# First dense layer of a two-layer transformer kernel: low weights of the last 64 features, two tiles in 64-row tiles of TensorE, and three PSUM banks dealt out by last use

## The chip, the cores and the metric

The kernel runs on one core of a Trainium2 chip. The metric is device time in microseconds (us), smaller is better. The kernel before takes 2498.18 us (median of three runs, 2494.75 to 2499.65). TensorE is PE in the profile, its weight loads are PEld, VectorE is DVE, ScalarE is ACT, GpSimd is POOL, and SP is the engine that issues most DMAs.

## The reference

Two transformer layers share one set of weights. Each is a linear attention with a learned softmax feature map, and a dense part with a squared ReLU:

```python
x = A_x                                                   # 1 x 2048 x 576
x = x + _A_ref(_layernorm(x, axis=-1), A_wqkv, A_w_phi, A_wo)
x = x + _B_ref(_layernorm(x, axis=-1), B_w1, B_b1, B_w2, B_b2)
x = x + _A_ref(_layernorm(x, axis=-1), A_wqkv, A_w_phi, A_wo)
x = x + _B_ref(_layernorm(x, axis=-1), B_w1, B_b1, B_w2, B_b2)

def _B_ref(x, w1, b1, w2, b2):                            # w1: 576 x 4608, w2: 4608 x 576
    h = jnp.einsum("bsd,df->bsf", x, w1) + b1
    r = jnp.where(h > 0, h, 0)
    h = r * r
    return jnp.einsum("bsf,fd->bsd", h, w2) + b2
```

The change touches only the first product of `_B_ref`, x @ w1.

## The kernel before

**Precision.** TensorE multiplies values of reduced precision (`float32r`) in one pass. Every factor is therefore split into a high and a low part, and a product is the sum of three: high by high, high by low, low by high.

**Blocks.** The 2048 rows are four blocks of 512 (`TB`). In the trace, `m_2ph` is the first product of block 2, both layers together. `g_mlp` is the dense part of one block and is called eight times: in layer 0 for the blocks 3, 2, 0, 1, in layer 1 for 1, 0, 3, 2. It is a generator, and `weave` runs one slot of other work (attention of the next block, norms, keys and values) after each of its `yield`s. The order on each engine is the order in which the program is written.

**Tiles of the dense part.** The 4608 hidden units are 36 tiles of 128 (`NF`). For a tile `f`, `hidden(f)` multiplies w1's columns by the transposed input and sums in a PSUM bank `ph`; `square(f)` applies ReLU and square on ACT (line 980 reads `ph`, line 981 squares in place in an SBUF tile `hr`) and splits the result on DVE into `hb` (lines 984 and 985); `second(f)` multiplies by w2 and sums in five banks `acc` that are held for the whole block (15 matmuls, lines 1000 and 992). On TensorE the order is hidden(f), second(f-1), hidden(f+1), second(f), and so on, with the slots of other work between them.

**The 576 features.** They are four chunks of 128 (`KC` = 4) and a rest of 64 (`DT`). `x["h"]` and `x["l"]` are the high and low input, features down the partitions. For the rest, `x["h"][:, KC]` holds the high part in one half of its 128 partitions and the low part in the other half. `load_twice` brings the 64 rows of w1 into both halves of the weight tile. So a matmul with the high weights `h1[:, KC]` gives high by high and high by low at once, and one with the low weights `l1[:, KC]` gives low by high, and low by low besides. A tile has 4 x 3 + 2 = 14 matmuls of 512 columns (line 975).

**Weights.** In the first block of layer 0 they are split on the chip and written to DRAM (`fresh`). In the seven others `first(f)` loads `h1` and `l1` of a tile in one DMA of 640 KB (line 938, on SP's queue), and `first2(f)` w2's (line 950, 576 KB). The tag `h1` has two buffers: the load for tile f+1 waits until hidden(f-1) has read its own.

**PSUM.** There are eight banks: five `acc`, one `h` for `ph` (except of f = 1), and a pool `ps_w` of two that `wtile` gives in turn to all other work.

Of the kernel before, what the change touches and what calls it, by code (L numbers as in the profile page):

```python
# [7 lines left out]
F32 = mybir.dt.float32  # L8
F32R = mybir.dt.float32r
AF = mybir.ActivationFunctionType  # L10
# [3 lines left out]
P = 128  # L14
TB = 512
# [6 lines left out]
def layers_kernel(  # L22
# [18 lines left out]
    nc = tc.nc  # L41
# [5 lines left out]
    NB = S // TB  # L47
    NF = F // P
    KC = D // P
    DT = D - KC * P  # L50
# [14 lines left out]
    ps_w = ctx.enter_context(tc.tile_pool(name="ps_w", bufs=2, space=bass.MemoryType.PSUM))  # L65
# [14 lines left out]


    spare = {"tags": [], "i": 0}

    def wtile(name):
        n = len(spare["tags"])
        spare["i"] += 1
        i = spare["i"] % (n + 2)
        if i < n:
            return ps_a.tile([P, TB], F32, tag=spare["tags"][i], name=name)
        return ps_w.tile([P, TB], F32, tag="w", name=name)  # L90

    def drain(gen):
        for _ in gen:
# [231 lines left out]
    class Norm:  # L325
# [62 lines left out]
        def rest(self, h):  # L388
            xh = self.dst["h"]
            rows = slice(h * TB // 2, (h + 1) * TB // 2)  # L390
            pt = wtile(f"{self.name}p{NT}{h}")
            for i in range(NT // 2):
                nc.tensor.transpose(pt[:DT, i * P : (i + 1) * P], self.xd[:, h * NT // 2 + i], ident)
            nc.scalar.activation(xh[:DT, KC, rows], pt[:DT, : TB // 2], AF.Copy)
            nc.vector.tensor_sub(xh[DT:, KC, rows], pt[:DT, : TB // 2], xh[:DT, KC, rows].bitcast(F32))

    class TripNorm(Norm):

# [55 lines left out]
        def rest(self, h):  # L454
            if not self.tails:
                return super().rest(h)
            xh = self.dst["h"]
            rows = slice(h * TB // 2, (h + 1) * TB // 2)
            own, far = (slice(i * DT, (i + 1) * DT) for i in (h, 1 - h))
            src = self.ends(h).rearrange("p (t g r) -> p t g r", t=2, g=KC)  # L460
            hi, lo = (xh[z, KC, rows].rearrange("p (t r g) -> p t g r", t=2, g=KC) for z in (own, far))
            nc.scalar.activation(hi, src, AF.Copy)
            nc.vector.tensor_sub(lo, src, hi.bitcast(F32))

    XT = (("h", xth, 0, KC // 2), ("l", xtl, 0, KC // 2), ("h", xth, KC // 2, NC), ("l", xtl, KC // 2, KC))

# [153 lines left out]
    def key_blocks(layer):  # L620
        kv = sums[layer]["kv"]
        last, w = NG - 1, gw[-1]
        kbh = cst.tile([GW, 2, D], F32R, name=f"kbh{layer}", tag="kbh")
        kbl = cst.tile([GW, 2, D], F32R, name=f"kbl{layer}", tag="kbl")
        sums[layer]["kb"] = kbh, kbl
        own = sb.tile([P, KC * P], F32, tag="xn", name=f"kq{layer}")
        own = own[:, : 2 * w].rearrange("p (s q f) -> p s q f", s=2, q=NQ)
        nc.vector.tensor_mul(own, kv[:, :, HG].unsqueeze(2).to_broadcast([P, 2, NQ, DH]),
                             quarter.unsqueeze(1).unsqueeze(3).to_broadcast([P, 2, NQ, DH]))
        blocks, todo = own, []  # L630

        def own_blocks():
            pt = wtile(f"kt{layer}2")
            p3 = pt[:w, : 2 * w].rearrange("p (s n) -> p s n", s=2)
            for s in range(2):
                nc.tensor.matmul(p3[:, s], blocks[:, s].rearrange("p q f -> p (q f)"),
                                 place.rearrange("p q d -> p (q d)"), start=True, stop=True)
            todo.append((p3, [k[:w, :, last * GW :] for k in (kbh, kbl)]))
            return todo

        for s in range(2):
            pt = wtile(f"kt{layer}{s}")
            nc.tensor.transpose(pt[:GW, :P], kv[:, s, :HG].rearrange("p j f -> p (j f)"), ident)
            own = sb.tile([P, TB], F32, tag="hr", name=f"ko{layer}{s}", bufs=2)
# [265 lines left out]
    def g_mlp(layer, b, x, after, name, fresh, apart, final):  # L910

        acc, parts, raw2 = [], {}, {}
        R = D - P
# [38 lines left out]

        every = slice(0, TB)

        def bank(f):
            parts[f] += (ps_w.tile([P, TB], F32, tag="w", name=f"{name}ph{f}") if f == 1 else
                         ps_a.tile([P, TB], F32, tag="h", name=f"{name}ph{f}"),)

        def hidden(f, cols):
            if len(parts[f]) == 3:  # L960
                bank(f)
            h1, l1, s2, ph = parts[f]
            xh, xl = x["h"], x["l"]
            todo = []
            for c in range(NC):
                ops = [(0, h1[:, c], xh[:, c, cols]), (1, l1[:, c], xh[:, c, cols])]
                if c < KC:
                    ops.insert(1, (0 if cols == every else 2, h1[:, c], xl[:, c, cols]))
                if c == KC and cols != every:
                    ops = [(3, *op[1:]) for op in ops]  # L970
                todo += ops
            if fresh or cols != every:
                todo.sort(key=lambda op: op[0])
            for k, (_, a, m) in enumerate(todo):
                nc.tensor.matmul(ph[:, cols], a, m, start=(k == 0), stop=(k == 3 * KC + 1))  # L975

        def square(f):
            s2, ph = parts[f][2:]
            hr = sb.tile([P, TB], F32, tag="hr", name=f"{name}hr{f}", bufs=2)
            nc.scalar.activation(hr, ph, AF.Relu, bias=b1t[:, f : f + 1])  # L980
# [28 lines left out]

        halves = (slice(0, TB // 2), slice(TB // 2, TB))  # L1010
        if apart:
            if fresh:
# [21 lines left out]
        second(0)  # L1034
        if fresh:
            load(3)
        first(2)
# [20 lines left out]
        yt = sb.tile([P, TB], F32, tag="hr", name=f"{name}yt", bufs=2)  # L1058
# [355 lines left out]
    def between(rows, held):  # L1414

        spare.update(tags=["h", "acc4", "acc1", "acc2", "acc3"], i=4)
        xprev, es, vpair, kpair = held["x"], held["es"], held["v"], held["k"]
        x = {}
        norm = Norm(x, "n1_last")
# [38 lines left out]
    def body():  # L1458
# [3 lines left out]
        for layer in range(2):  # L1462
            q1 = None
            ready, prev_rows, keep = {}, None, {}
            for i, b in enumerate(order):
                n = f"{layer}_{b}"
                nxt, rows = {}, []
                gen = g_mlp(layer, b, ready, rows, f"m{n}", layer == 0 and i == 0, i == 0, layer == 1 and i == NB - 1)
# [112 lines left out]
```

## Time and profile before

| | |
|---|---|
| median of 3 runs | 2498.18 us (2494.75 to 2499.65) |
| profiled execution | 2497.19 us, of which the span 2495.5 us |
| PE busy | 2478.5 us, 14968 matmuls |
| PEld busy | 2182.9 us |
| DVE, ACT, POOL busy | 1260.1, 788.1, 189.4 us |
| DMA | 545.07 MB, mean 218 GB/s |

The first number of a row of the timeline is the start in us from the start of the span, the second the length of the merged run, then engine, source line, operation, written tile <- read tiles, forms, and how many instructions were merged; in brackets stands the idle time of the engine just before it and what ended it. The time outside the span is 1.7 us.

### The profile page before, as it was taken

To read this page: it belongs to the slowest core of one execution; us is meant where nothing else is said; L and a number is where in the kernel's file an instruction comes from. 1 tells how busy PE (TensorE), PEld (TensorE's weight loads), DVE (VectorE), ACT (ScalarE), POOL (GpSimd) and SP (SyncE) were. 2 spreads that over 40 slices of the span, in tenths; PEclk is the share of its full clock that TensorE was granted. 3 is DMA by queue.
4 is the path that set the end of the run, shared out by engine and by line. 5 is a ranking of instruction groups with operands and counts; after the bars stand their busy time and mean duration, and the time that the engine had idled before them with its cause. 6 is when DMAs were issued, how large, how long until landed. Compare 5 with 4: busy or idle time off the path is not lost.

```text
span 2495.5 us, 37635 instructions
## 1 busy us (share of the span) xinstructions
PE 2478.5 (99%) x14968; PEld 2182.9 (87%) x14968; DVE 1260.1 (50%) x2214; ACT 788.1 (32%) x1439; POOL 189.4 (8%) x539
## 2 busy tenths in 40 slices
PE   9999999999999999999999999999999999999999
PEld 8999888888888888888888988888888888888887
DVE  6679885545744476455113776433453436442112
ACT  5444453422232223223213332413233222312212
POOL 4211100000200001000000011000110002000000
PEclk9999999999999999999999999999999999999999
DMA  9313698986767677684565248678576867676565
GB/s 321 98 54 92 243 315 266 310 315 205 259 229 271 217 206 273 216 298 146 195 199 182 92 141 263 209 217 291 186 257 204 261 219 246 217 230 230 194 199 171
DMA packets 214374, 545.07 MB, mean 218 GB/s; under 512 B 29006, under 2 KB 96814, under 8 KB 214198
## 3 DMA queue, kind: packets, MB, share of 16 engines
q1 hardware_dynamic: 163638, 500.44, 60.8%
q10 hardware_dynamic: 50560, 42.21, 5.3%
q8 instruction: 119, 1.95, 0.3%
q14 instruction: 57, 0.47, 0.1%
HBM read 439.20 MB, written 103.38 MB: 217 GB/s over the span
## 4 chain that ended last, share of the span: by engine, by line
PE 95%; DMA 2%; DVE 1%; ACT 1%; issue 1%; SPq 0%; ACTq 0%; DVEq 0%
PE m_1ph L975 9%; PE m_3ph L975 9%; PE m_0ph L975 9%; PE m_2ph L975 9%; PE m_1acc L1000 7%; PE m_3acc L1000 7%; PE m_2acc L1000 7%; PE m_0acc L1000 7%; PE m_1acc L992 2%; PE m_3acc L992 2%; PE m_2acc L992 2%; PE m_0acc L992 2%; PE a_0po L816 1%; PE a_2po L816 1%; PE kvp L593 1%; PE a_3po L816 1%
## 5 line engine op out<-in xcount | busy, mean ns | idle before, releaser
L975 PE MATMUL m_2ph<-a_2nh,m_2h 128*128 128x512 f32 x720 | 225.2, 394 | 1.2 <-ACT m_2hr L980 0.7
L975 PE MATMUL m_0ph<-a_0nh,m_0h 128*128 128x512 f32 x720 | 225.0, 394 | 1.3 <-ACT m_0hr L980 1.1
L1000 PE MATMUL m_3acc<-m_3s,m_3hb 128*128 128x448 f32 x864 | 189.3, 367 | 0.4 <-DVE m_3hb L984 0.4
L1000 PE MATMUL m_1acc<-m_1s,m_1hb 128*128 128x448 f32 x864 | 189.0, 367 | 0.3 <-PE m_1ph L975 0.3
L1000 PE MATMUL m_2acc<-m_2s,m_2hb 128*128 128x448 f32 x864 | 188.9, 367 | 0.0
L1000 PE MATMUL m_0acc<-m_0s,m_0hb 128*128 128x448 f32 x864 | 188.8, 367 | 0.0
L984 DVE CAST m_2hb<-m_2hr 128x512 fp32r<-128x512 f32 x72 | 31.2, 433 | 292.4 <-ACT m_2hr L981 292.3
L1000 PEld LDWEIGHTS m_1acc<-m_1s,m_1hb 128*128 128x128 f32 x864 | 161.9, 188 | 18.8 <-PE m_1ph L975 0.5
L1000 PEld LDWEIGHTS m_3acc<-m_3s,m_3hb 128*128 128x128 f32 x864 | 161.2, 188 | 17.8 <-PE m_3ph L975 0.6
L1000 PEld LDWEIGHTS m_2acc<-m_2s,m_2hb 128*128 128x128 f32 x864 | 161.6, 188 | 17.2
L1000 PEld LDWEIGHTS m_0acc<-m_0s,m_0hb 128*128 128x128 f32 x864 | 161.6, 188 | 17.2
L975 PEld LDWEIGHTS m_2ph<-a_2nh,m_2h 128*128 128x128 f32 x720 | 135.3, 188 | 32.7 <-ACT m_2hr L980 1.2
L975 PEld LDWEIGHTS m_0ph<-a_0nh,m_0h 128*128 128x128 f32 x720 | 135.2, 188 | 32.8 <-ACT m_0hr L980 1.5
L984 DVE CAST m_1hb<-m_1hr 128x512 fp32r<-128x512 f32 x72 | 30.7, 427 | 258.8 <-ACT m_1hr L981 258.8
L980 ACT ACTIVATE m_2hr<-m_2ph,b1t 128x512 f32<-128x512 f32 x72 | 49.6, 689 | 339.1 <-PE m_2ph L975 327.4
L980 ACT ACTIVATE m_1hr<-m_1ph,b1t 128x512 f32<-128x512 f32 x72 | 49.6, 689 | 319.1 <-PE m_1ph L975 309.1
L980 ACT ACTIVATE m_0hr<-m_0ph,b1t 128x512 f32<-128x512 f32 x72 | 49.6, 689 | 317.2 <-PE m_0ph L975 288.6
L984 DVE CAST m_0hb<-m_0hr 128x512 fp32r<-128x512 f32 x72 | 31.5, 438 | 229.0 <-ACT m_0hr L981 229.0
L984 DVE CAST m_3hb<-m_3hr 128x512 fp32r<-128x512 f32 x72 | 31.7, 440 | 173.6 <-ACT m_3hr L981 173.6
L980 ACT ACTIVATE m_3hr<-m_3ph,b1t 128x512 f32<-128x512 f32 x72 | 49.6, 689 | 219.3 <-PE m_3ph L975 209.2
L975 PE MATMUL m_3ph<-t0onh,m_3h 128*128 128x512 f32 (+1 forms) x380 | 112.9, 384 | 0.6 <-ACT t0onh L385 0.5
L975 PE MATMUL m_1ph<-t1onh,m_1h 128*128 128x512 f32 (+1 forms) x380 | 112.4, 382 | 0.8 <-ACT t1onh L385 0.5
(2050 smaller groups left out, 5734.9 us busy)
## 6 DMA issues: line engine op xcount, KB each, us to landing
m_2h<-dw SPq DMA_DIRECT2D x72, 640.0 KB
m_0h<-dw SPq DMA_DIRECT2D x72, 640.0 KB
m_1h<-dw SPq DMA_DIRECT2D x72, 640.0 KB
m_2s<-dw SPq DMA_DIRECT2D x72, 576.0 KB
m_0s<-dw SPq DMA_DIRECT2D x72, 576.0 KB
m_1s<-dw SPq DMA_DIRECT2D x72, 576.0 KB
dw<-m_3h SPq DMA_DIRECT2D x36, 640.0 KB
m_3h<-dw SPq DMA_DIRECT2D x36, 640.0 KB
```

The lines of the kernel that those rows point to most:

```text
L593: nc.tensor.matmul(po[32 * q : 32 * q + 32, :, j], vt[:, h * VW : h * VW + 32], e[:, :, h * DH : (h + 1) * DH], start=not stay, stop=True, ...
L816: nc.tensor.matmul(pt[:, :HP], a, m[:w, g], start=(g == 0 and k == 0), stop=(g == NG - 1 and k == 2))
L975: nc.tensor.matmul(ph[:, cols], a, m, start=(k == 0), stop=(k == 3 * KC + 1))
L980: nc.scalar.activation(hr, ph, AF.Relu, bias=b1t[:, f : f + 1])
L984: nc.vector.tensor_copy(hh, hr)
L992: nc.tensor.matmul(acc[KC], a, m, start=(f == 0 and k == 0), stop=(f == NF - 1 and k == 2))
L1000: nc.tensor.matmul(acc[t][:, :R], a[:, rows], m, start=(f == 0 and k == 0), stop=(f == NF - 1 and k == 2))
```

## The change

**Pairs.** For most even f from 2 on, `hidden(f)` leaves out the last matmul of its tile, the one with `l1[:, KC]`, and so does `hidden(f+1)`. In their place stand two matmuls at the end of hidden(f), one for each of the two tiles: 64 rows of weights each, the one for tile f in partitions 0 to 63, the one for f+1 in partitions 64 to 127. They write different banks. The low weights of both tiles multiply the high input alone; the product of low by low, which the matmul before gave besides, is left out in these tiles. Since the second of the two opens the sum of tile f+1, that tile's bank is taken, and its `l1` is read, at the end of hidden(f).

**The input of the pairs.** `twice` copies the high half of the last 64 features into both halves of a new tile `xt`, in four copies on POOL, once in a block, after second(0). `dst[h]` notes in which half the high part lies.

**Which tiles.** 17 pairs in each of the four blocks of layer 1, 16 (without f = 10) in the last three blocks of layer 0, none in its first: 116 pairs. 232 matmuls of 128 rows are replaced by 232 of 64.

**Banks and buffers.** `h` and the pool's two become three banks in a list; a taker gets the one whose last use was longest ago, `wtile` puts it back at once, `square` after its ReLU. `hr` has one buffer in place of two; `xt` has the room.

```diff
+    banks = ["w0", "w1"]
+
+    def take_bank(name):
+        tag = banks.pop(0)
+        return tag, ps_a.tile([P, TB], F32, tag=tag, name=name)
...
-        return ps_w.tile([P, TB], F32, tag="w", name=name)
+        tag, pt = take_bank(name)
+        banks.append(tag)
+        return pt
...
+        def twice():
+
+            xt = both["x"] = sb.tile([P, TB], F32R, tag="xt", name=f"{name}xt", bufs=1)
+            for h in range(2):
+                cols = slice(h * TB // 2, (h + 1) * TB // 2)
+                for i in range(2):
+                    nc.gpsimd.tensor_copy(xt[i * DT : (i + 1) * DT, cols], x["h"][x[h], KC, cols].bitcast(F32))
...
-        def hidden(f, cols):
-            if len(parts[f]) == 3:
+        def hidden(f, cols, pair=None):
+            if f not in ph:
                 bank(f)
...
+                elif pair is not None:
+                    ops.pop()
...
-                nc.tensor.matmul(ph[:, cols], a, m, start=(k == 0), stop=(k == 3 * KC + 1))
+                nc.tensor.matmul(ph[f][:, cols], a, m, start=(k == 0 and pair != 1), stop=(k == n and pair != 0))
+            if pair == 0:
+                bank(f + 1)
+                for i in range(2):
+                    rows = slice(i * DT, (i + 1) * DT)
+                    nc.tensor.matmul(ph[f + i], parts[f + i][1][rows, KC], both["x"][rows], start=(i == 1), stop=(i == 0))
...
-            hr = sb.tile([P, TB], F32, tag="hr", name=f"{name}hr{f}", bufs=2)
-            nc.scalar.activation(hr, ph, AF.Relu, bias=b1t[:, f : f + 1])
+            hr = sb.tile([P, TB], F32, tag="hr", name=f"{name}hr{f}", bufs=1)
+            nc.scalar.activation(hr, ph.pop(f), AF.Relu, bias=b1t[:, f : f + 1])
             nc.scalar.activation(hr, hr, AF.Square)
+            banks.append(held.pop(f))
...
-            hidden(f, every)
+            hidden(f, every, 0 if f in pairs else 1 if f - 1 in pairs else None)
...
+                pairs = [f for f in range(2, NF, 2) if layer or i and f != 10]
```

PE of block 2 in layer 0, from the last matmuls of hidden(2) to the first of hidden(3); `ph2` and `ph3` are the sums of these tiles, `h` and `l` behind `a0_2n` the high and low input, `h1_2` the weights of tile 2. Before:

```order
L975 MATMUL m0_2ph2_6341<-a0_2nl_5710,m0_2h1_2_6316 128x512
L975 MATMUL m0_2ph2_6341<-a0_2nh_5709,m0_2h1_2_6316 128x512 x3
L1000 MATMUL m0_2acc0_6296<-m0_2s2_1_6254,m0_2hb1_6274 128x448 x3
L1000 MATMUL m0_2acc1_6297<-m0_2s2_1_6254,m0_2hb1_6274 128x448 x3
L1000 MATMUL m0_2acc2_6298<-m0_2s2_1_6254,m0_2hb1_6274 128x448 x3
L1000 MATMUL m0_2acc3_6299<-m0_2s2_1_6254,m0_2hb1_6274 128x448 x3
L992 MATMUL m0_2acc4_6300<-m0_2hb1_6274,m0_2s2_1_6254 128x512 x3
L384 MATMUL n1_3p0_6385<-ident_221,n1_3n0_6325 128x128 x4
L975 MATMUL m0_2ph3_6405<-a0_2nh_5709,m0_2h1_3_6339 128x512
```

The same place in the changed kernel; `m0_2xt` is the copied high input:

```order
L995 MATMUL m0_2ph2_6343<-a0_2nl_5707,m0_2h1_2_6318 128x512
L995 MATMUL m0_2ph2_6343<-a0_2nh_5706,m0_2h1_2_6318 128x512 x2
L1000 MATMUL m0_2ph2_6343<-m0_2xt_6313,m0_2h1_2_6318 128x512
L1000 MATMUL m0_2ph3_6357<-m0_2xt_6313,m0_2h1_3_6341 128x512
L1026 MATMUL m0_2acc0_6293<-m0_2s2_1_6251,m0_2hb1_6271 128x448 x3
L1026 MATMUL m0_2acc1_6294<-m0_2s2_1_6251,m0_2hb1_6271 128x448 x3
L1026 MATMUL m0_2acc2_6295<-m0_2s2_1_6251,m0_2hb1_6271 128x448 x3
L1026 MATMUL m0_2acc3_6296<-m0_2s2_1_6251,m0_2hb1_6271 128x448 x3
L1018 MATMUL m0_2acc4_6297<-m0_2hb1_6271,m0_2s2_1_6251 128x512 x3
L390 MATMUL n1_3p0_6389<-ident_218,n1_3n0_6327 128x128 x4
L995 MATMUL m0_2ph3_6357<-a0_2nh_5706,m0_2h1_3_6341 128x512
```

The two rows of line 1000 stand in the place of one of the three last matmuls of tile 2; the second of them reads the weights of tile 3 (`h1_3`), 16 matmuls of the dense part and the slot of other work ahead of where tile 3 read them first. The last run of hidden(3), `x3` before, is `x2` now. Both rows have 64 rows of weights.

POOL at the start of the same block, where the four small norm operations of block 3's next layer stand (lines 359 and 360 before, 365 and 366 in the changed kernel):

```order
L365 TENSOR_SCALAR n1_3d0_6281<-n1_3m0_6280 128x1
L366 TENSOR_TENSOR n1_3d0_6281<-n1_3d0_6281,mhalf_244 128x1
L365 TENSOR_SCALAR n1_3d1_6289<-n1_3m1_6288 128x1
L366 TENSOR_TENSOR n1_3d1_6289<-n1_3d1_6289,mhalf_244 128x1
L974 CAST m0_2xt_6313<-a0_2nh_5706 64x256 x4
L365 TENSOR_SCALAR n1_3d2_6337<-n1_3m2_6336 128x1
L366 TENSOR_TENSOR n1_3d2_6337<-n1_3d2_6337,mhalf_244 128x1
```

The row of line 974 is new; the other rows stood in this order before. SP issues the same DMAs in the same order.

More of the change, by code (lines that the diff above doesn't have):

```diff
@@ L64, in layers_kernel @@
     sb = ctx.enter_context(tc.tile_pool(name="sb", bufs=2))
-    ps_w = ctx.enter_context(tc.tile_pool(name="ps_w", bufs=2, space=bass.MemoryType.PSUM))
     ps_a = ctx.enter_context(tc.tile_pool(name="ps_a", bufs=1, space=bass.MemoryType.PSUM))
@@ L395, in rest @@
             nc.vector.tensor_sub(xh[DT:, KC, rows], pt[:DT, : TB // 2], xh[:DT, KC, rows].bitcast(F32))
+            self.dst[h] = slice(0, DT)
     class TripNorm(Norm):
@@ L463, in rest @@
             nc.vector.tensor_sub(lo, src, hi.bitcast(F32))
+            self.dst[h] = own
     XT = (("h", xth, 0, KC // 2), ("l", xtl, 0, KC // 2), ("h", xth, KC // 2, NC), ("l", xtl, KC // 2, KC))
@@ L643, in key_blocks @@
             nc.tensor.transpose(pt[:GW, :P], kv[:, s, :HG].rearrange("p j f -> p (j f)"), ident)
-            own = sb.tile([P, TB], F32, tag="hr", name=f"ko{layer}{s}", bufs=2)
+            own = sb.tile([P, TB], F32, tag=("hr", "xt")[s], name=f"ko{layer}{s}", bufs=1)
             own = own[:GW, : NQ * GW].rearrange("p (q j d) -> p q j d", q=NQ, j=HG)
@@ L908, in plan_attend, with g_mlp @@
         plan_norm(plan, norm, out.project, [at + t for t in range(NT)], scales, turns, [at + 5 + more, at + 7 + more])
-    def g_mlp(layer, b, x, after, name, fresh, apart, final):
+    def g_mlp(layer, b, x, after, name, fresh, apart, final, pairs):
         acc, parts, raw2 = [], {}, {}
@@ L953, in g_mlp @@
         every = slice(0, TB)
+        ph, held, both = {}, {}, {}
         def bank(f):
-            parts[f] += (ps_w.tile([P, TB], F32, tag="w", name=f"{name}ph{f}") if f == 1 else
-                         ps_a.tile([P, TB], F32, tag="h", name=f"{name}ph{f}"),)
-        def hidden(f, cols):
-            if len(parts[f]) == 3:
+            held[f], ph[f] = take_bank(f"{name}ph{f}")
+        def twice():
[6 more added lines that the diff above has]
+            if f not in ph:
                 bank(f)
-            h1, l1, s2, ph = parts[f]
+            h1, l1 = parts[f][:2]
             xh, xl = x["h"], x["l"]
@@ L973, in hidden @@
                 todo.sort(key=lambda op: op[0])
+            n = len(todo) - 1
             for k, (_, a, m) in enumerate(todo):
-                nc.tensor.matmul(ph[:, cols], a, m, start=(k == 0), stop=(k == 3 * KC + 1))
+                nc.tensor.matmul(ph[f][:, cols], a, m, start=(k == 0 and pair != 1), stop=(k == n and pair != 0))
[4 more added lines that the diff above has]
+                    nc.tensor.matmul(ph[f + i], parts[f + i][1][rows, KC], both["x"][rows], start=(i == 1), stop=(i == 0))
         def square(f):
-            s2, ph = parts[f][2:]
-            hr = sb.tile([P, TB], F32, tag="hr", name=f"{name}hr{f}", bufs=2)
-            nc.scalar.activation(hr, ph, AF.Relu, bias=b1t[:, f : f + 1])
+            s2 = parts[f][2]
+            hr = sb.tile([P, TB], F32, tag="hr", name=f"{name}hr{f}", bufs=1)
+            nc.scalar.activation(hr, ph.pop(f), AF.Relu, bias=b1t[:, f : f + 1])
             nc.scalar.activation(hr, hr, AF.Square)
+            banks.append(held.pop(f))
             hb = sb.tile([P, 2 * D], F32R, tag="hb", name=f"{name}hb{f}")
@@ L1011, in g_mlp @@
         if apart:
+            banks.insert(0, "h")
             if fresh:
@@ L1034, in g_mlp @@
         second(0)
+        if pairs:
+            twice()
         if fresh:
@@ L1057, in g_mlp @@
         features(NF - 1)
-        yt = sb.tile([P, TB], F32, tag="hr", name=f"{name}yt", bufs=2)
+        yt = sb.tile([P, TB], F32, tag="hr", name=f"{name}yt", bufs=1)
         nc.scalar.activation(yt, acc[KC], AF.Copy)
@@ L1416, in between @@
         spare.update(tags=["h", "acc4", "acc1", "acc2", "acc3"], i=4)
+        banks.remove("h")
         xprev, es, vpair, kpair = held["x"], held["es"], held["v"], held["k"]
@@ L1467, in body @@
                 nxt, rows = {}, []
-                gen = g_mlp(layer, b, ready, rows, f"m{n}", layer == 0 and i == 0, i == 0, layer == 1 and i == NB - 1)
+                pairs = [f for f in range(2, NF, 2) if layer or i and f != 10]
+                gen = g_mlp(layer, b, ready, rows, f"m{n}", layer == 0 and i == 0, i == 0, layer == 1 and i == NB - 1,
+                            pairs)
                 plan = Plan()
```

## The prediction

> **What bounds the kernel now.** First the page: the engines' shares, the granted clock, and the chain that ended last.
>
> ```profile
> span 2495.5 us, 37635 instructions
> PE 2478.5 (99%) x14968; PEld 2182.9 (87%) x14968; DVE 1260.1 (50%) x2214; ACT 788.1 (32%) x1439; POOL 189.4 (8%) x539
> PEclk9999999999999999999999999999999999999999
> PE 95%; DMA 2%; DVE 1%; ACT 1%; issue 1%; SPq 0%; ACTq 0%; DVEq 0%
> ```
>
> TensorE is busy from end to end at full clock, and the chain runs 95% through it. So what a change adds to or takes from TensorE's stream, idle time included, goes into the time at its full length. Next, what a matmul costs there: the groups by form, and the timeline inside one tile.
>
> ```profile
> L975 PE MATMUL m_2ph<-a_2nh,m_2h 128*128 128x512 f32 x720 | 225.2, 394 | 1.2 <-ACT m_2hr L980 0.7 <-DMA m_2h<-dw 0.5
> L975 PEld LDWEIGHTS m_2ph<-a_2nh,m_2h 128*128 128x128 f32 x720 | 135.3, 188 | 32.7 <-ACT m_2hr L980 1.2 <-issue 1.1
> 1205.12 0.39 PE L975 MATMUL m_1ph<-a_1nh,m_1h 128*128 128x512 f32 x1
> 1205.12 0.19 PEld L975 LDWEIGHTS m_1ph<-a_1nl,m_1h 128*128 128x128 f32 x1
> 1205.35 0.39 PE L975 MATMUL m_1ph<-a_1nl,m_1h 128*128 128x512 f32 x1
> 1205.57 0.62 PE L975 MATMUL m_1ph<-a_1nh,m_1h 128*128 128x512 f32 x2
> 1206.03 0.39 PE L975 MATMUL m_1ph<-a_1nl,m_1h 128*128 128x512 f32 x1
> ```
>
> A matmul of 512 columns lasts 394 ns, but the next one starts 0.23 us after it (1205.12, 1205.35, 1205.57): the pipeline overlaps them, and 0.23 is the price of one. The weights of the next matmul load (188 ns) from the very start of the matmul ahead (1205.12 on both engines), so a load costs nothing. That cover is what the change may lose.
>
> **The saving.** 116 pairs replace two matmuls by two that might run at once. If the pair costs as much as one, each saves 0.23 us: 26.7 us in all.
>
> **The switch of tile shape.** The pair uses 64 of the array's 128 rows for each matmul. Before, only two kinds of matmul use part of the array: the keys' matmuls on 32 columns (line 593), and a single matmul with one row of weights (line 586), which runs twice. The timeline around the latter, TensorE and its weight loads:
>
> ```profile
> 56.05 0.29 PE L493 MATMUL s03pv<-w0v1h,n_0h 128*128 128x288 f32 x1
> 56.18 0.29 PE L493 MATMUL s03pv<-w0v1l,n_0h 128*128 128x288 f32 x1
> 56.40 0.39 PE L586 MATMUL kvp<-zero 1*128 1x288 f32 x1
> 56.73 0.47 PE L593 MATMUL kvp<-s0K0e,s00v 128*32 128x36 f32 x32
> ...
> 56.05 0.19 PEld L493 LDWEIGHTS s03pv<-w0v1l,n_0h 128*128 128x128 f32 x1
> 56.40 0.18 PEld L586 LDWEIGHTS kvp<-zero 1*128 1x128 f32 x1 [0.16 <-issue]
> ```
>
> At 56.05 a weight load starts with the matmul ahead, as everywhere. The load for the one-row matmul starts only at 56.40, 0.22 after the last full matmul began, though it waits for nothing that the profile shows ("issue"). The array runs empty first. The matmul then lasts 0.39 in place of 0.29: its own load, 0.10, is no longer hidden. The next change of shape costs the same again: 56.40 to 56.73 is the 0.10 and another 0.22. The way into and out of the 32-column shape, from 512 columns and back to full ones:
>
> ```profile
> 609.22 0.86 PE L975 MATMUL m_2ph<-a_2nh,m_2h 128*128 128x512 f32 x3
> 610.01 0.77 PE L593 MATMUL kv_0k<-k_3K0e,v_3v 128*32 128x36 f32 x64
> 610.63 0.76 PE L593 MATMUL kv_1k<-k_3K1e,v_3v 128*32 128x36 f32 x64
> ...
> 79.22 0.40 PE L493 MATMUL s05pv<-w0v0h,n_1h 128*128 128x288 f32 x1
> 79.45 0.29 PE L493 MATMUL s05pv<-w0v0l,n_1h 128*128 128x288 f32 x1
> 79.22 0.19 PEld L493 LDWEIGHTS s05pv<-w0v0h,n_1h 128*128 128x128 f32 x1
> 79.33 0.19 PEld L493 LDWEIGHTS s05pv<-w0v0l,n_1h 128*128 128x128 f32 x1
> ```
>
> The last of the three starts at 609.22 + 2 x 0.23 = 609.68; the next shape begins 0.33 later (610.01). The way back again shows a first matmul of 0.40 and a next load 0.11 after the first: the exposed load. So a switch after a matmul of 512 columns costs 0.33 to the weight load and 0.10 until the stream begins, where 0.23 is usual.
>
> [...]
>
> **The pair, step by step.** From the start of the last full matmul of hidden(f): 0.33 to the pair's first load, 0.10 until its stream begins, 0.01 for the second stream, 0.33 to the next full load, 0.10 until that stream: 0.87. Before, two matmuls stood there: 0.46. That is 0.41 more in tile f; tile f+1 has one matmul less, 0.23. Net **+0.18 us per pair, +20.9 us** for 116.
>
> The 0.01 is the one step without a row of 64-row tiles. Near it: 64 matmuls of 36 columns start within 610.63 - 610.01 = 0.62 us, 0.010 each, where 36 columns in turn would need 0.016 at 0.23 per 512. So neighbouring tiles of the array do overlap, loads included. The bounds: the second load behind the first, +0.10; the two streams in turn, +0.23. I take the overlap, as nearest. The switch itself is bounded by nothing (no drain for 64 rows) and the rows above; I take the rows, since one of the two kinds is of rows too.
>
> **The weights of tile f+1 are read earlier.** The pair needs `l1` of f+1 at the end of hidden(f), not at the start of hidden(f+1): second(f-1), 15 matmuls or some 3.1 us at 0.23 per 512 columns, and the slot's work earlier. Its load still waits for hidden(f-1). TensorE takes its instructions in order, so a late load holds second(f-1) and all behind it. In a quiet stretch there is room: issued at 1202.14, the load is through when the DMA engines fall quiet, at most 3.9 us later, and the pair comes 28 matmuls of 448 and 512 columns after the issue, some 6 us at 0.23 per 512.
>
> ```profile
> 1202.14 0.32 SPq L938 DMA_DIRECT2D m_1h<-dw  x1
> 1205.00:1205.50 0.50, 0.50 (x4) 0.41 (x3) 0.00 (x0) 0.00 (x0) 0.00 (x0) 1.00 0.60 246
> 1205.50:1206.00 0.50, 0.50 (x4) 0.41 (x3) 0.00 (x0) 0.00 (x0) 0.00 (x0) 1.00 0.14 33
> ```
>
> Where other loads share the queue there is none. Two such places of layer 1, with the next block's weights (line 310) in between:
>
> ```profile
> 2174.18 0.34 SPq L938 DMA_DIRECT2D m_3h<-dw  x1
> 2179.64 0.85 PE L975 MATMUL m_3ph<-a_3nh,m_3h 128*128 128x512 f32 x3
> 2183.95 0.47 PE L975 MATMUL m_3ph<-a_3nh,m_3h 128*128 128x512 f32 x1 [0.33 <-DMA m_3h<-dw]
> ...
> 1625.67 0.34 SPq L938 DMA_DIRECT2D m_1h<-dw  x1
> 1629.22 0.78 SPq L310 DMA_DIRECT2D a_0o1l<-kept_ol  x2
> 1631.13 0.85 PE L975 MATMUL m_1ph<-t1onh,m_1h 128*128 128x512 f32 x3
> 1634.96 0.39 PE L975 MATMUL m_1ph<-t1onh,m_1h 128*128 128x512 f32 x1
> ```
>
> In the first, tile f+1 waits for its weights until 2183.95 even now. The pair's streams would begin 0.43 after the last full matmul (2179.64 + 0.23), at 2180.30: a wait of 3.6 us. In the second the same queue stands; TensorE does not wait at 1634.96, so the weights are there by then, and the wait is at most 3.4; I take 3. For the other pairs I add 3.4 as an estimate, halfway between nothing and a wait of 0.06 in each: **+10**, with bounds 3.6 and 15. The other waits of this kind, in layer 0, are in the tiles after f = 10, which is not paired.
>
> **The copies on POOL.** Nearest row: a cast of 288 columns, 0.42; for 256 columns 0.38, four make 1.5.
>
> ```profile
> L259 POOL CAST w0v0h<-fv 128x288 fp32r<-128x288 f32 x5 | 2.1, 423 | 0.0
> 532.06 0.65 POOL L360 TENSOR_TENSOR n_3d<-n_3d,mhalf 128x1 f32<-128x1 f32 x1
> 532.79 0.85 PE L975 MATMUL m_2ph<-a_2nh,m_2h 128*128 128x512 f32 x3
> 1113.43 0.65 POOL L360 TENSOR_TENSOR n_0d<-n_0d,mhalf 128x1 f32<-128x1 f32 x1
> 1114.09 0.85 PE L975 MATMUL m_1ph<-a_1nh,m_1h 128*128 128x512 f32 x3
> ```
>
> In layer 0 the copies queue behind the norm's operation that ends at 532.71, so they end at 534.2; the first pair's streams could begin at 532.79 + 0.23 + 0.43 = 533.45. A wait of 0.8, in three blocks (the last: 1115.6 against 1114.75): **+2.5**, between 0 and 4. In layer 1 no norm stands ahead, and hidden(2) hides the copies.
>
> **Edits at nothing.**
>
> ```profile
> L980 ACT ACTIVATE m_2hr<-m_2ph,b1t 128x512 f32<-128x512 f32 x72 | 49.6, 689 | 339.1 <-PE m_2ph L975 327.4
> ```
>
> Banks: ACT reads `ph` in 0.69 us after hidden ends, under second(f-1)'s 3.1 us; the rotation gives a bank that was used two takes ago, so I count nothing, and 2 us if ACT is late where a slot takes two banks. One `hr` buffer: DVE must have read it before second(f) starts, which is also when hidden(f+1) ends and the next ReLU may begin. The same cover serves both; without it ACT would wait for DVE, and TensorE for both only if they were late by more than second(f-1)'s 3.1 us.
>
> **Sum.** 2497.2 (the profiled execution) + 20.9 + 10 + 2.5 = 2530.6, rounded to **2531**. The median of the runs is 1.0 above the profiled execution, well inside the rounding of the terms.
>
> **The rivals.**
> - *No drain for 64 rows.* A pair then costs 0.24 in place of two times 0.23: -0.22 x 116 = -25.5, with the waits of POOL and DMA 0.2 longer where they occur, +14: 2486. For it: the largest saving on an engine that is 99% busy. Against it: both partial shapes in the trace drain, both ways, each time. It decides in favour of the change when the way in and out costs less than 0.22 - 12.5 / 116 = 0.11 us per pair. [...] No row here shows a pair without a switch.
> - *Only one way drains:* without the way out's 0.33 and 0.10 the next full stream begins 0.23 after the pair: 0.67 - 0.46 - 0.23 = -0.02 per pair, 2497.2 - 2.3 + 12.5 = 2507.
> - *Loads one behind the other:* +0.09 x 116 = 10.4: 2541.
> - *The two do not run side by side,* and the change does not do what it says: the second stream 0.23 behind the first, +0.22 x 116 = 25.5: 2556.
>
> **How the numbers follow.** Chances: my forecast 0.61 (2521 to 2537 by the bounds of its waits), loads in turn 0.10, streams in turn 0.06, one-way drain 0.06, no drain 0.17. The range 2505 to 2556 takes in all but the last and part of the streams in turn. A measurement of this kernel tells about 0.2%, 5 us, from no change. Faster holds no drain except its upper end, 0.16; same that end and the lower part of the one-way drain, 0.05; slower the rest, 0.79.
>
> **What would show it.** In the timeline after: the load of the first 64-row matmul 0.33 after the last full matmul (right) or with it (wrong, 2486); the two 64-row matmuls 0.01 or 0.1 to 0.2 apart; the matmul behind them some 0.4 later and 0.1 longer than its kind; among the waits, the second 64-row matmul on DMA of `h1`, together about 10, and the first on POOL in three blocks. Wrong would make it above all a drain that does not occur or is much shorter between 128 and 64 rows.

## The result and the profile after

| | before | after |
|---|---|---|
| median | 2498.91 us (2494.75 to 2499.97, 4 runs) | 2543.71 us (2540.66 to 2545.57, 4 runs) |
| ratio | | 1.0185, 95% interval 1.0173 to 1.0197 |
| profiled execution | 2497.19 us | 2545.57 us |

The change makes the kernel 44.8 us slower. The forecast was 2531 (2505 to 2556): the direction is right, the time lies in the range, and 12.7 us are missing. The time alone does not confirm the mechanism: 2543.7 lies outside the 2521 to 2537 that the prediction gave its own forecast, and only 2.7 us from its rival "loads one behind the other" (2541). So the traces have to decide. From the page of the changed kernel: the span, the engines' busy time, TensorE's granted clock and the chain's shares:

```profile
span 2543.8 us, 37766 instructions
PE 2505.9 (99%) x14968; PEld 2155.9 (85%) x14968; DVE 1262.4 (50%) x2214; ACT 788.8 (31%) x1439; POOL 201.0 (8%) x567
PEclk9999999999999999999999999999999999999999
PE 94%; DMA 3%; DVE 1%; ACT 1%; issue 1%; POOL 0%; SPq 0%; DVEq 0%; ACTq 0%; POOLq 0%
```

TensorE is still the bound. It is 27.4 us longer "busy" with as many matmuls, though its weight loads are 27 us shorter; and 48.3 - 27.4 = 20.9 us of the longer span are new idle time. So there are two places to look: what a pair does to the stream, and the waits.

The timeline of a pair in block 1, TensorE first, then its weight loads (start, length, engine, line, operation, tiles, form, count, idle before):

```profile
1232.30 0.63 PE L995 MATMUL m_1ph<-a_1nh,m_1h 128*128 128x512 f32 x2
1232.85 0.50 PE L1000 MATMUL m_1ph<-m_1xt,m_1h 64*128 64x512 f32 x2
1233.28 2.72 PE L1026 MATMUL m_1acc<-m_1s,m_1hb 128*128 128x448 f32 x12
...
1232.07 0.41 PEld L995 LDWEIGHTS m_1ph<-a_1nh,m_1h 128*128 128x128 f32 x2
1232.85 0.19 PEld L1000 LDWEIGHTS m_1ph<-m_1xt,m_1h 64*128 64x128 f32 x2 [0.36 <-issue]
1233.28 0.71 PEld L1026 LDWEIGHTS m_1acc<-m_1s,m_1hb 128*128 128x128 f32 x4 [0.24 <-issue]
```

The last full matmul starts at 1232.30 + 0.23 = 1232.53. The pair's loads start 0.32 later, and both 64-row matmuls together last 0.50, hardly more than one full matmul with its load exposed. The next full load starts only 0.43 after the start of the pair. The median start-to-start times of all 116 pairs, from the records, are 327 ns from the last full matmul into the pair, 3 ns between its two matmuls, 426 ns out of it, and 312 ns to the matmul behind that, whose kind otherwise takes 205. So the two do run side by side (3 ns apart), the next load comes late both ways (the prediction's drain: 327 and 426 ns, where full matmuls of 512 columns follow each other in 231), and a load of 0.10 us is exposed (the last step's 107 ns). The sum counts the four steps (of the last the 107 ns above the usual 205) and takes off the three full matmuls of 0.231 that had stood there: 0.327 + 0.003 + 0.426 + 0.107 - 3 x 0.231 = 0.17 us net for a pair, 19.7 us for 116.

The waits of TensorE after (engine, tile, line <- what ended the wait: us in total, times, longest):

```profile
PE a_2pt L780 <- DVE a_2ol L806: 10.3, 4, 2.6
PE m_1ph L1000 <- DMA m_1h<-dw: 2.5, 2, 1.4
PE m_3ph L1000 <- DMA m_3h<-dw: 2.4, 1, 2.4
...
PE m_0ph L1000 <- DMA m_0h<-dw: 1.2, 1, 1.2
PE t0opn L801 <- DVE t0of L719: 1.2, 1, 1.2
...
PE t0opt L717 <- DVE t0ool L806: 0.9, 1, 0.9
...
PE m_0ph L1000 <- POOL m_0xt L974: 0.8, 1, 0.8
PE m_1ph L1000 <- POOL m_1xt L974: 0.8, 1, 0.8
PE m_2ph L1000 <- POOL m_2xt L974: 0.6, 1, 0.6
```

The rows of line 1000 are the two kinds of wait that the prediction named. The largest row was not foreseen: four waits of 2.6 us, all in block 3 of layer 0, which has no pairs, and at the attention's matmuls, which the change does not touch. Two more such waits stand ahead of layer 0's dense part (`t0opn`, `t0opt`), in what the kernel calls a barrier: the stretch between a layer's attention sums and its first dense block. What these instructions have in common is that their PSUM banks now come from the list.

### The profile page after: what moved, and what is told of

It reads as the page before. It is cut to its first block, busy times and chain, and to the rows that moved or that the text cites. A ratio compares the mean times of both kernels' runs of the same rounds, so it can differ in the third digit from the quotient of the medians.

```text
span 2543.8 us, 37766 instructions
## 1 busy us (share of the span) xinstructions
PE 2505.9 (99%) x14968; PEld 2155.9 (85%) x14968; DVE 1262.4 (50%) x2214; ACT 788.8 (31%) x1439; POOL 201.0 (8%) x567
## 4 chain that ended last, share of the span: by engine, by line
PE 94%; DMA 3%; DVE 1%; ACT 1%; issue 1%; POOL 0%; SPq 0%; DVEq 0%; ACTq 0%; POOLq 0%
PE m_2ph L995 8%; PE m_0ph L995 8%; PE m_3ph L995 8%; PE m_1ph L995 8%; PE m_3acc L1026 7%; PE m_1acc L1026 7%; PE m_2acc L1026 7%; PE m_0acc L1026 7%; PE m_3acc L1018 2%; PE m_2acc L1018 2%; PE m_0acc L1018 2%; PE m_1acc L1018 2%; PE a_0po L824 1%; PE a_2po L824 1%; PE kvp L601 1%
## 5 line engine op out<-in xcount | busy, mean ns | idle before, releaser
L995 PE MATMUL m_0ph<-a_0nh,m_0h 128*128 128x512 f32 x654 | 209.8, 394 | 1.0 <-DMA m_0h<-dw 1.0
L995 PE MATMUL m_2ph<-a_2nh,m_2h 128*128 128x512 f32 x654 | 210.0, 395 | 0.0
L995 PEld LDWEIGHTS m_0ph<-a_0nh,m_0h 128*128 128x128 f32 x654 | 122.8, 188 | 29.4 <-DMA m_0h<-dw 1.5
L995 PEld LDWEIGHTS m_2ph<-a_2nh,m_2h 128*128 128x128 f32 x654 | 122.9, 188 | 28.8 <-issue 0.4
L995 PE MATMUL m_0ph<-a_0nl,m_0h 128*128 128x512 f32 x288 | 113.1, 393 | 0.0
```

The costliest lines, as they stand in the source:

```text
L995: nc.tensor.matmul(ph[f][:, cols], a, m, start=(k == 0 and pair != 1), stop=(k == n and pair != 0))
```

## Experiments

Every ratio is against the kernel before, run beside it on the same chip. The diffs show the main lines; `...` marks what is left out.

**The list alone: no pairs.**

```diff
-                pairs = [f for f in range(2, NF, 2) if layer or i and f != 10]
+                pairs = []
```

> The changed kernel with an empty list of pairs: banks, buffers and their order as changed, every matmul as before, no copies on POOL. Theory (the dealing of banks costs time by itself, where a product is summed over two slots): the four waits of 2.58 us of the transposes for DVE in block 3 of layer 0 stay (10.3 us), and some 3 us in the two stretches between the layers' parts: 2498.9 + 13.4 = 2512 us. Rival (banks are free, the waits come with the pairs): 2499 us.

Measured: 2515.18 us (2508.06 to 2516.66), ratio 1.0067 (1.0051 to 1.0083). The list costs 17 to 18 us without a single pair (0.67% by the ratio, 18.2 between the medians). One place of this run beside the same place before: first the timeline of before, then TensorE, then VectorE of this run.

```profile
366.16 0.39 PE L793 MATMUL a_2pn<-a_2fh,kbl 126*126 126x512 f32 x1
366.39 0.27 PE L772 MATMUL a_2pt<-ident,a_2Q2e 128*126 128x128 f32 x1
...
364.55 0.40 PE L801 MATMUL a_2pn<-a_2fh,kbl 126*126 126x512 f32 x1
367.52 0.47 PE L780 MATMUL a_2pt<-ident,a_2Q2e 128*126 128x128 f32 x1 [2.58 <-DVE a_2ol L806]
367.86 3.89 PE L1026 MATMUL m_3acc<-m_3s,m_3hb 128*128 128x448 f32 x12
...
365.71 0.43 DVE L1010 CAST m_3hb<-m_3hr 128x512 fp32r<-128x512 f32 x1 [2.46 <-ACT m_3hr L1006]
366.17 0.69 DVE L1011 TENSOR_TENSOR m_3hb<-m_3hr,m_3hb 128x512 fp32r<-128x512 f32 x1
366.78 0.68 DVE L806 TENSOR_TENSOR a_2ol<-a_2pn,a_2oh 126x512 fp32r<-126x512 f32 x1
```

Before, the transposes `pt` follow the product `pn` at once. Here they wait until VectorE has read `pn` (line 806), and VectorE comes to that only after the square's two operations (lines 1010 and 1011). The addresses of the tiles in the two programs say why. A `pn` is summed over two slots (`times` for s = 0 and s = 1) and read after the second. `wtile` puts its bank back at the moment it is taken. Two takers later, while `pn` is still being read, the bank comes up again: `pn0` and `pt11` share bank 5, `pn1` and `pt21` bank 3, `pn2` and `pt31` bank 4, `pn3` and `pt41` bank 5, one for each of the four waits. So the list gives out the bank that was *taken* longest ago, and not, as the description above has it, the one whose last use was longest ago. In the kernel before the pool keeps track of what is still in use. It does not deal its two banks in turn either: while `pn` holds one bank, every `pt` gets the other.

Each such wait can cost more than itself. The windows of this run around the first of them (stretch, length, busy time of PE, PEld, DVE, ACT, POOL with counts, granted clock, DMA share, GB/s):

```profile
366.00:368.00 2.00, 0.48 (x3) 0.48 (x3) 1.97 (x5) 0.72 (x3) 0.00 (x0) 0.78 0.92 336
368.00:370.00 2.00, 2.00 (x7) 1.78 (x7) 0.49 (x2) 0.38 (x1) 0.00 (x0) 0.50 0.99 303
370.00:372.00 2.00, 2.00 (x10) 1.83 (x9) 0.00 (x0) 0.00 (x0) 0.00 (x0) 0.87 0.79 257
372.00:374.00 2.00, 2.00 (x11) 1.60 (x11) 0.81 (x2) 1.52 (x5) 0.00 (x0) 1.00 0.00 0
```

The granted clock falls to a half, and 2 x (0.22 + 0.50 + 0.13) = 1.7 us of clock are lost. This execution has three such stretches, and 10.3 (four waits) + 3 (waits in the two barriers) + 3 x 1.7 = 18.4 us, against 18.8 between this profiled execution (span 2514.3) and that of before (2495.5).

**The bank of `pn` held until it is read, no pairs.** `wtile` gets a list in which it leaves the bank, and `times` puts it back behind the operation on line 806:

```diff
-                self.pn[g] = wtile(f"{name}pn{g}")
+                self.kept = []
+                self.pn[g] = wtile(f"{name}pn{g}", self.kept)
...
                 nc.vector.tensor_sub(lo, pn[:w, :n], hi.bitcast(F32))
+                banks.extend(self.kept)
```

> The changed kernel without pairs, with pn's bank held until its sum has been read (e5's edit). Theory: the early return of pn's bank is the whole cost of the dealing but for the waits in the barriers, so the four waits of 2.58 us and the stretches at half clock behind them go, and 2497 + 3 = 2500 is left. Rival: three banks dealt from a list cost by themselves, 2508 or more.

Measured: 2501.62 us (2498.17 to 2506.80, 12 runs), ratio 1.0016 (1.0007 to 1.0025). The four long waits are gone and with them 13.6 us between the medians. What is left shows among the waits:

```profile
PE t0opn L805 <- DVE t0of L722: 1.2, 1, 1.2
...
PE t1opo L829 <- DVE t1oolt L810: 0.9, 1, 0.9
...
PE t1opt L720 <- DVE t1of L722: 0.6, 1, 0.6
PE t0opo L829 <- DVE t0ox L832: 0.6, 1, 0.6
```

All are in the barriers, and together 3.3 us. Two causes were possible: the one buffer of `hr`, or once more the list.

**The buffers alone, in the kernel before.**

```diff
-            own = sb.tile([P, TB], F32, tag="hr", name=f"ko{layer}{s}", bufs=2)
+            own = sb.tile([P, TB], F32, tag=("hr", "xt")[s], name=f"ko{layer}{s}", bufs=1)
...
-            hr = sb.tile([P, TB], F32, tag="hr", name=f"{name}hr{f}", bufs=2)
+            hr = sb.tile([P, TB], F32, tag="hr", name=f"{name}hr{f}", bufs=1)
...
-        yt = sb.tile([P, TB], F32, tag="hr", name=f"{name}yt", bufs=2)
+        yt = sb.tile([P, TB], F32, tag="hr", name=f"{name}yt", bufs=1)
```

> The kernel of before with two things of the change alone: hr has one buffer in place of its tag's ring, and the blocks' ko tiles carry their own tag. Theory (the prediction's edit at nothing): free, 2497 to 2498. Rival: hr's one buffer holds the evictions back in the barriers and is what makes the waits of some 3 us there, 2500 to 2501; then the page shows waits of t0opn and t0opt of about 1 us each, as after.

Measured: 2496.20 us (2494.12 to 2500.14, 11 runs), ratio 0.9995 (0.9986 to 1.0003), and no `t0opn` among the waits. The one buffer costs nothing, as predicted.

**The bank `h` joins the list later, with the held bank and no pairs.** By the addresses, in the barrier `t0opt10` and `t0opn0`, taken one right behind the other, get the same bank 3. The generator of the dense part puts `h` at the head of the list when it is started; at that point the barrier's ring of spare banks still holds `h` too, and has just given it out.

```diff
         if apart:
-            banks.insert(0, "h")
             if fresh:
...
             yield
+            banks.insert(0, "h")
             for f in range(2):
                 hidden(f, halves[0])
```

> e9 (no pairs, pn's bank held) and the bank h joins the list only where the dense part takes it, after the generator's first step, in place of at the generator's start, when the barrier's ring of spare banks still deals it out too. Theory: the wait of 1.16 us in each barrier is for that bank, which the ring gives to a pt and the list to pn right behind it; without it the list costs nothing, 2497 to 2498.5, and t0opn no longer waits for L722. Rival: hr and xt or the list itself cause the rest, 2501 as e9.

Measured: 2496.75 us (2494.02 to 2498.34, 11 runs), ratio 0.9991 (0.9982 to 1.0000). The timelines of this place, TensorE and VectorE of the changed kernel, then TensorE of this run:

```profile
245.83 0.27 PE L717 MATMUL t0opt<-ident,t0q3Q3e 128*126 128x128 f32 x1
247.26 0.73 PE L801 MATMUL t0opn<-t0of,kbh 126*126 126x256 f32 x2 [1.16 <-DVE t0of L719]
...
246.12 1.08 DVE L719 TENSOR_TENSOR t0of<-t0opt,t0of 126x256 fp32r<-126x256 f32 x3
...
246.48 0.27 PE L720 MATMUL t0opt<-ident,t0q3Q3e 128*126 128x128 f32 x1
246.79 0.84 PE L805 MATMUL t0opn<-t0of,kbh 126*126 126x256 f32 x2
```

In the changed kernel `pn` starts when VectorE has read the last of three `pt` (246.12 + 1.08 = 247.20); here it starts 0.31 after the transposes. So with these two repairs the third bank and the list cost nothing.

**The same repairs with the pairs.** First the held bank alone:

> The changed kernel, but the bank of a product that is summed over two slots (line 798 of the changed kernel) goes back to the list only when its sum has been read, as the pool of before did it. Theory (those banks are dealt out again while they wait for DVE): without the four waits of 2.58 us, 2543.7 - 10.3 = 2533 us, down to 2530 if the waits between the parts go too. Rival (the one buffer of hr, or the third bank itself): 2544 us. It may also be that too few banks are left while a pair holds one: then above 2544.

Measured: 2530.86 us (2529.70 to 2536.33), ratio 1.0140 (1.0125 to 1.0155); the four waits are gone, `t0opn` is still there. Then both repairs:

> The changed kernel with the same two repairs of the dealing (pn's bank held, h joins later). It is the sum of the prediction without a cost of the banks. Theory: 2527 to 2529, e5 less what e9 lost to e10; the switch of shape, the early weights and the copies are left, about 30 us above before. Rival: the waits that go here come back at the pairs, 2531 as e5.

Measured: 2529.19 us (2524.94 to 2531.82), ratio 1.0125 (1.0110 to 1.0141). The two intervals overlap, so the step from one repair to two isn't shown by the times of these kernels; `t0opn` is gone from the waits, and others have grown a little. The waits of the kernel with both repairs, without those that before has too:

```profile
PE m_3ph L1005 <- DVE m_3hb L1015: 2.0, 1, 2.0
...
PE m_0ph L1005 <- POOL m_0xt L979: 0.9, 1, 0.9
PE m_2ph L1005 <- POOL m_2xt L979: 0.8, 1, 0.8
PE m_1ph L1005 <- POOL m_1xt L979: 0.8, 1, 0.8
PE m_3ph L1000 <- DMA m_3h<-dw: 0.8, 1, 0.8
PE m_0ph L1000 <- DMA m_0h<-dw: 0.8, 1, 0.8
```

This is the kernel that the prediction's sum describes: 30.4 us above before, where the sum had 33.4. By the starts of its profiled execution, the switch is 19.7 us again, the late weights are 5.8 and the copies 4.1, together 29.6, against 29.9 between the two profiled executions. The dealing is worth 2543.71 - 2529.19 = 14.5 us.

The row of 2.0 us is a wait for weights too, though the profile puts it down to VectorE. In the program the pair's second matmul waits for VectorE only until `pn4` has been read, which is done before VectorE's idle time ahead of 2198.1. The last part of the weights' DMA lands at 2205.07, and the matmul starts at 2205.20. In the changed kernel the same pair starts the same 0.14 behind its DMA (2225.04 and 2225.17).

**Both low matmuls at the pair's place, but with all 128 rows.** Nothing switches, and the copies are left out; only the early reading of the weights of tile f+1 is left, beside the list.

```diff
-                    nc.tensor.matmul(ph[f + i], parts[f + i][1][rows, KC], both["x"][rows], start=(i == 1), stop=(i == 0))
+                    nc.tensor.matmul(ph[f + i], parts[f + i][1][:, KC], xh[:, KC], start=(i == 1), stop=(i == 0))
...
-        if pairs:
-            twice()
```

> The two matmuls of a pair at the same place, but with all 128 rows of weights and the input as before, no copies on POOL: no change of tile shape, nothing saved, weights needed as early, banks as changed. Theory (the switch of shape costs 0.17 us net per pair): 2543.7 - 19.7 (switch) - 3.7 (POOL) = 2520 us, waits for DMA of about 10 us stay. Rival (the switch is cheap and the early need of the weights and the order are dear): 2535 to 2544 us.

Measured: 2522.10 us (2516.54 to 2526.60), ratio 1.0107 (1.0090 to 1.0123). Against the list alone the early reading costs 6.9 us; from here to the changed kernel it is 21.6 us for switch and copies.

**One 64-row matmul alone, in the kernel before.** In the 116 tiles with a pair's first half, the last matmul uses only rows 0 to 63. It leaves out the product with the other half of the rows.

```diff
+            if f in singles:
+                _, a, m = todo.pop()
+                todo.append((4, a[:DT], m[:DT]))
```

> The kernel before, with one edit: in 116 tiles the last matmul of the tile uses the rows 0 to 63 alone, where that half holds the low input it computes low by low in the place of low by high. No pairs, no early weights, banks as before. Theory (each visit to the 64-row shape costs 0.33 + 0.10 in and 0.33 + 0.10 out in place of 2 x 0.23): + 0.40 x 116 = 46 us, 2545 us. Rival (64 rows alone cause no drain; the drain comes from two matmuls to two banks, or from the early weights): 2499 us.

Measured: 2539.65 us (2539.05 to 2540.83), ratio 1.0173 (1.0158 to 1.0188). The weight loads around it:

```profile
1232.02 0.41 PEld L978 LDWEIGHTS m_1ph<-a_1nh,m_1h 128*128 128x128 f32 x2
1232.80 0.18 PEld L978 LDWEIGHTS m_1ph<-a_1nh,m_1h 64*128 64x128 f32 x1 [0.36 <-issue]
1233.23 2.35 PEld L1003 LDWEIGHTS m_1acc<-m_1s,m_1hb 128*128 128x128 f32 x12 [0.25 <-issue]
```

The way out takes 1233.23 - 1232.80 = 0.43 with one matmul as with two. So the visit alone costs: by the starts (327, 429 and 312 ns) 0.327 + 0.429 + 0.107 - 2 x 0.231 = 0.40 us, 46 us for 116, of which 42.5 show in the time; where the rest goes is open. The second matmul of a pair starts 3 ns behind the first, which takes 0.23 back.

**Both matmuls in the same rows.**

```diff
-                    rows = slice(i * DT, (i + 1) * DT)
+                    rows = slice(0, DT)
```

> Both matmuls of a pair in the rows 0 to 63, where they cannot run at once; all else as in the changed kernel. Theory (the two run side by side in the changed kernel): the second starts 0.22 us later, less where it waits for DMA anyhow: + 24 us, 2568 us. Rival (they ran in turn already): 2544 us.

Measured: 2563.07 us (2559.74 to 2564.40), ratio 1.0265 (1.0247 to 1.0282).

```profile
1253.44 0.73 PE L1000 MATMUL m_1ph<-m_1xt,m_1h 64*128 64x512 f32 x2
1254.11 1.08 PE L1026 MATMUL m_1acc<-m_1s,m_1hb 128*128 128x448 f32 x4
```

The two now last 0.73 in place of 0.50, and the next load comes 0.67 after them, in place of 0.43. By the median starts (327, 342, 320 and 308 ns) working side by side saves 0.23 a pair, 27 us; 19.4 show between the medians. In this profiled execution the second matmuls of the pairs also wait 8.5 us less for weights and copies (2.5 in place of 11.0 by the starts). The longer pair hides a part of that; the rest is weights that came earlier in this execution, which no run explains.

**The pair twice.** It adds the pair's products a second time.

```diff
-                for i in range(2):
-                    rows = slice(i * DT, (i + 1) * DT)
-                    nc.tensor.matmul(ph[f + i], parts[f + i][1][rows, KC], both["x"][rows], start=(i == 1), stop=(i == 0))
+                for k in range(4):
+                    i, rows = k % 2, slice(k % 2 * DT, (k % 2 + 1) * DT)
+                    nc.tensor.matmul(ph[f + i], parts[f + i][1][rows, KC], both["x"][rows], start=(k == 1), stop=(k == 2))
```

> Each pair is issued twice in a row, four matmuls of 64 rows in one visit to the shape (the pair's products are added twice). Theory (within the shape two matmuls cost one, and the switch is paid once): + 0.23 x 116 = 27 us, less where the second pair hides under a wait, 2568 us. Rival (the two do not overlap): + 0.46 x 116 = 53 us, 2597 us. Rival (each change of row group drains): + 0.8 x 116, 2640 us.

Measured: 2575.07 us (2574.14 to 2578.33), ratio 1.0317 (1.0301 to 1.0332).

```profile
1251.91 0.73 PE L1000 MATMUL m_1ph<-m_1xt,m_1h 64*128 64x512 f32 x4
1252.57 0.67 PE L1026 MATMUL m_1acc<-m_1s,m_1hb 128*128 128x448 f32 x2
```

The visit takes 0.66 in place of 0.43: a second pair costs 0.23, as much as one full matmul in place of two. By that a visit with two pairs would just pay for itself: 0.17 + 0.23 - 2 x 0.23 = -0.06 us, a small gain as an estimate. That would need the sums of four tiles open at once; it wasn't tried. The time is 31.4 us above the changed kernel's, where 116 x 0.23 = 27. This profiled execution has seven half-clock periods and the changed kernel's two (mean clock 0.995 and 0.999); how much of the difference they make was not separated.

**As few waits as possible.** The held bank, the copies at the start of the block, and 108 pairs, without those whose weights came late.

```diff
             for f in range(2):
...
+            if pairs:
+                twice()
...
-                pairs = [f for f in range(2, NF, 2) if layer or i and f != 10]
+                late = {(0, 1): (10, 34), (0, 2): (10, 34), (0, 3): (10,), (1, 0): (12, 16, 24), (1, 1): (26,),
+                        (1, 2): (26, 34)}.get((layer, i), ())
+                pairs = [f for f in range(2, NF, 2) if (layer or i) and f not in late]
```

> As e5, with the copies on POOL issued at the start of a block, ahead of the norm's operations, and without the eight pairs whose second weights came late or near it; 108 pairs stay. Theory (all that is then left is the switch, 0.17 us net per pair): 2498.9 + 108 x 0.17 = 2517 us. Rival (waits move to other pairs, or the rest has another cause): 2524 us or more. If pairs gained by themselves, it would fall below 2499.

Measured: 2521.60 us (2519.88 to 2523.99), ratio 1.0099 (1.0084 to 1.0114), between the theory's 2517 and the rival's 2524. The switch alone is 108 x 0.17 = 18.4 of the 24.6 us. The waits taken away did not all go: others stand in their place, such as one of 1.2 us for w2's weights in block 0. No version with pairs came near the kernel before, and none of the others beats it.

## Why the prediction was right, and where it was short

| step | predicted | found |
|---|---|---|
| switch of shape, 116 pairs | 20.9 | 19.7, by the starts |
| late weights of tile f+1 | 10 (3.6 to 15) | 9.7 by the starts, 5.8 with both repairs; 6.9 by the runs without a switch |
| copies on POOL | 2.5 (0 to 4) | 3.8 by the starts, 4.1 with both repairs |
| one `hr` buffer | 0 | 0 |
| banks | 0 (2 if ACT is late) | 14.5 |

**The switch.** Each piece came as written: 0.33 in, nothing between the two, 0.33 and the exposed 0.10 out, 0.10 again behind. The rows of the one-row and the 32-column shape, taken from elsewhere in the trace of before, held for 64 rows. That they would was the author's estimate: the trace of before has no matmul with 64 rows. In that trace these two shapes start 0.224 us after the last matmul of 288 columns, and the 32-column shape 0.32 after one of 512; at 0.231 per 512 columns the streams ahead take 0.130 and 0.231, so the load comes 0.09 behind the stream in either case, and 0.10 at the pair (0.327). That refuted four rivals: no drain, only one way, loads in turn, and streams in turn. The 0.003 between the pair's starts refutes the last two; the run in the same rows shows the 0.34 that it would have been.

The case for the drain was weaker than the prediction had it. It counts two kinds of matmul that use part of the array, and says that both drain each time. There are more, among them the 44 transposes with 64 columns of weights (line 393), and they don't:

```profile
543.44 0.60 PE L384 MATMUL n_3p<-ident,n_3n 128*128 128x128 f32 x4
543.88 0.38 PE L393 MATMUL n_3p<-ident,n_3e 128*64 128x128 f32 x2
544.01 0.47 PE L975 MATMUL m_2ph<-a_2nh,m_2h 128*128 128x512 f32 x1
```

They follow full transposes at the usual 0.11 (of four within 543.44 + 0.60, the last starts at 543.77), and the next full matmul starts 0.03 after the second of them, as it does behind the transposes with 126 columns. Why this shape goes without a drain no run tests. That 64 rows drain by themselves rests on the run with one 64-row matmul alone (0.43 us to the next full load).

**The late weights.** By the starts, the two places that the prediction named waited 2.9 us (3.6 were predicted) and 1.9 (3), and six of the other pairs together 4.8 (3.4). That they add up to almost the 10 of the sum is luck: two terms were too large and the third too small, and in the kernel with both repairs they add up to 5.8. The waits view shows less, since it counts only the idle time.

**The copies.** Three waits on the first 64-row matmul, as predicted, 2.4 us by the starts. The second waits 0.45 more in each of the three blocks, since its copies end later; the sum had left that out.

**The step that failed** is the first of the edits at nothing: "the rotation gives a bank that was used two takes ago, so I count nothing". It asked when ACT is done with `ph`, and so looked at one kind of taker only. It took "used two takes ago" for "free", which holds for a tile that is filled and read in one slot. `pn` is held over two slots, and `h` was in two lists at once. The bound of 2 us was for the wrong reader: it was VectorE's reading of `pn` behind its work for the dense part. Of the 14.5 us the four waits are 10.3 and those in the barriers 3. That the rest is half-clock stretches (two in the profiled execution, 1.7 us each) is argued and not shown, since their number differs between executions. The range took all this in only because it was wide enough for the rivals.

What stays open: how late the weights come at a pair differs between executions and kernels (9.7 and 5.8 us in all), and no run sets apart what decides it.

## What to carry to other kernels

Two matmuls of half the rows, in different rows, ran at once here (3 ns apart), but the visit to their shape had a price of its own (0.63 us; a lone matmul takes 0.23 of it back, a pair 0.46); count how many pairs share a visit before packing. When a pool that knows what is live is replaced by a list, ask of each taker when its *last reader* is done, not when it was taken, and whether a bank can stand in two lists. And test the side edits without the main one: here the part that had nothing to do with the pairs cost a third of the loss.

## What the runs showed of the hardware that was not expected

**Behind some waits the granted clock was 0.50 for 3.41 us.** In the run of the list alone the 12 matmuls of 448 columns at 367.86, behind a wait of 2.58 us, took 3.89 us where 12 of the same kind took 2.72 at full clock (at 1233.28 in the changed kernel). The changed kernel's profiled execution has two stretches at 0.50, from 247.36 and 380.48 us on, each of 3413 ns in the trace's record of the clock; between them and behind them, up to 2544, the clock is 1.00. So of its four waits of 2.58 us it shows a fall behind one, the second; the other fall follows waits of 0.51 and 1.16 us. How often the clock falls differs between executions of one program: the twelve runs without pairs and with the held bank hint at this in their times, since the three with a mean clock of 0.999 are the three longest (2504.6 to 2506.8).

The two stretches start 133.12 us apart, 39 times 3.4133. Cut into pieces of that length from there, the profile has TensorE idle for 1.67 us (0.51 and 1.16) in the piece ahead of the first fall and for 2.22 in the one ahead of the second. The three waits of 2.58 us without a fall are split between two pieces; the most idle time in one of these is 1.88. Whether this is what decides, no run tests.

**Two 64-row matmuls in the same rows start further apart than two full ones.** Full matmuls of 512 columns start 0.23 us apart; two 64-row matmuls in the same rows, in the run above, start 342 ns apart by the records, 0.11 more. In different rows it is 3 ns.
